# Packed attention and a low-rank mixer on one core: three moves at the change from attention to the products

## The chip, the cores and the metric

The kernel runs on one core of one Trainium2 chip. The core has five engines that work side by side and meet through semaphores: TensorE (PE in the profile; PEld is its loading of weights), VectorE (DVE), ScalarE (ACT), GpSimd (POOL) and SyncE (SP), which here only issues the loads and stores; 16 DMA engines carry these out. The metric is the device time of one execution in microseconds (us).

## The reference

```
p_packed = softmax(p k^T / 8) v             # 8 batches, 8 heads: 32 packed tokens from 576
x        = softmax(q p_packed^T / 8) p_packed   # 576 tokens again, heads side by side: 576 x 512
u        = x + (mix of the tokens of x by U V)  # U 576 x 32, V 32 x 576
out      = u + relu(u w1) w2                # w1 512 x 2048, w2 2048 x 512
```

q, k and v are 8 x 8 x 576 x 64 in float32. U, V, w1 and w2 come as float64; the kernel makes float32 of them on the chip, from the two halves of their bits (`float32_of`, L71 to L82): an absolute value on ScalarE (L77) and four integer operations on VectorE (L78 to L81) for each piece.

## The kernel before

**Products.** Every large product runs as three matmuls on a high and a low part (`mm3`, L84 to L88): high by high, high by low, low by high. So each operand is split: ScalarE writes the high part, VectorE or GpSimd the difference.

**First stage.** The first attention (packed tokens from k and v) runs over 16 units, a unit being one batch and four of its heads (loop at L521). The loop writes for unit i: the turn of the exponentials of unit i-1 and the scores of unit i on TensorE, the loads of `vt` for i+1 and `kx` for i+2, the maximum and exponential, conversions of w1, the product with v for unit i-2 (`a_pack`) and the turn of its result (`a_heads`, unit i-3). Beside it, from unit 4 on, three steps a unit of the second attention of batch 0 (`attention`, L255, a list of 24 steps from `load` to the last `mix2`). U and V are loaded (`load_uv`) and prepared (`prepare_uv`) at units given by two conditions, L544 and L546. At unit 13 stands the first fold of w1 with the packed tokens (`fold`: 16 matmuls, casts L378, differences L379), at unit 14 the loads of w2's first pieces, the `q` loads of batch 1, and the conversion of w2's piece 0. What is written here is put in order by a scheduler that simulates the engines; each engine then works through its own list in that order.

**Second stage.** From L567 on the order is as written. For each batch and each of 16 columns kt: a first product `gemm1` (L86 to L88 into `h_ps`, then ReLU on ScalarE, L619, and the difference `hl` on VectorE, L622), one step of the next batch's attention, the second product `gemm2` of column kt-1 with something in between its halves, every fourth column a fold, and another step. In batch 0 the four remaining pieces of the first attention (`rest`) go in between the halves of columns 1 to 4, and w2 is converted piece by piece while it is used: `split_w2` (cast L160, difference L161), the load of a later piece, `convert_w2`.

What sets the places of batch 1's steps is a list into which empty steps are put:

```
w2x = convert_w2(1)
for n in (20, 19, 18, 15, 15, 14, 13, 12, 12, 11, 5, 0, 0, 0, 0):
    steps.insert(n, lambda: None)
```

**Buffers.** `bank()` hands out two PSUM banks in turn (named `t_ps`), shared by the turns, the scores of the second attention, the folds and `mix1`/`mix2`. `x_tile` has two buffers, used by U and V, by the `q` loads and by the tokens that `mix1` reads; `bits` has two, `vt` three. A new user of a buffer waits until the last reader of the old one is done.

Of the kernel before, what the change touches and what calls it, by code (L numbers as in the profile page):

```python
# [19 lines left out]
def packed_attention_mixer_kernel(  # L20
# [50 lines left out]
    def float32_of(x, t, raw, out=None, tested=False):  # L71


        low, high = raw[:, :, 0], raw[:, :, 1]
        out = x if out is None else out.bitcast(I32)
        if not tested:
            nc.scalar.activation(t, high.bitcast(F32), AF.Abs)  # L77
        nc.vector.tensor_single_scalar(t, t, LEAST, op=ALU.max)  # L78
        nc.vector.tensor_scalar(x, t.bitcast(I32), 3, 0x3FFFFFF8, op0=ALU.logical_shift_left, op1=ALU.bitwise_and)
        nc.vector.scalar_tensor_tensor(x, high, -0x40000000, x, op0=ALU.bitwise_and, op1=ALU.bitwise_or)  # L80
        nc.vector.scalar_tensor_tensor(out, low, 29, x, op0=ALU.logical_shift_right, op1=ALU.bitwise_or)  # L81
        return out.bitcast(F32)  # L82
# [44 lines left out]
    def conv_tile(dtype):  # L127
        return pipe.tile([P, DM], dtype, name="os", bufs=4)
# [7 lines left out]
    def load_w1(n):  # L136
        x, c = chunks[n]
        b = bits["w1", n] = bits_tile() if n % 2 else sA.tile([P, 512, 2], I32, name="bits2")
        nc.sync.dma_start(out=b.rearrange("p x t -> p (x t)"), in_=w1[P * x:P * x + P, 2 * QW * c:2 * QW * c + 2 * QW])
# [15 lines left out]
    def convert_w2(kt):  # L155
        return kt, float32_of(conv_tile(I32), conv_tile(F32), bits.pop(("w2", kt)))
# [238 lines left out]
    def bank_a(tag):  # L395
        return lambda: psA.tile([P, 512], F32, name=f"{tag}_ps", tag=tag)

    def a_load(u):
        b, g = UN[u]
        ua[u] = {}  # L400
        if g == 0:
            pn[b] = sA.tile([P, 2, D], F32, name="pn", bufs=1)
            nc.sync.dma_start(out=pn[b], in_=p[b].rearrange("(g h) n d -> (h n) g d", g=2))
        ua[u]["x"] = sA.tile([P, 2 * S], F32, name="kx", bufs=3)
        load_nat(ua[u]["x"], k, b, g)

    def a_load_v(u):
        b, g = UN[u]
        vt = ua[u]["v"] = sT.tile([P, 5, 4 * D], F32, name="vt", bufs=3)
        rows = v[b, 4 * g:4 * g + 4].rearrange("h (i c) d -> i c h d", c=NT)  # L410
        main = v[b, 4 * g:4 * g + 4].rearrange("h (i c) d -> i h (c d)", c=NT)
        for a in range(2):
            nc.sync.dma_start(out=vt[:, :4].rearrange("(i a) h x -> a i h x", a=2)[a],
                              in_=main[:, :, 4 * D * a:4 * D * a + 4 * D])
        nc.sync.dma_start(out=vt[:64, 4].rearrange("p (h d) -> p h d", h=4), in_=rows[:, 8])
# [13 lines left out]
    def a_turn(u):  # L429
        b, g = UN[u]  # L430
        if g == 0:
            a_p(b)
        ua[u]["t"] = sA.tile([P, 4, 5 * I], F32, name="kT")
        for h in range(3):
            turn(ua[u]["t"], ua[u]["x"], h, bank_a("k"), split=h == 1)

    def a_scores(u):
        b, g = UN[u]
        s_ps = psA.tile([P, 1024], F32, name="s_ps", tag="s", bufs=1)
        scores(pT[b], ua[u]["t"], g, (s_ps[:, 512 - 5 * I:512], s_ps[:, 512:512 + 4 * I]))  # L440
        ua[u]["s"] = s_ps[:, 512 - 5 * I:512 + 4 * I]

    def a_softmax(u):
        b, g = UN[u]
        if g == 0:
            sums[b] = sT.tile([P, 4], F32, name="sm", bufs=3)
        mx = sums[b][:, 2 + g:3 + g]
        nc.vector.tensor_reduce(mx, ua[u]["s"], axis=AX.X, op=ALU.max, negate=True)
        e1 = ua[u]["e"] = sT.tile([P, S], F32, name="e1")
        nc.scalar.activation(e1, ua[u]["s"], AF.Exp, bias=mx, accum_out=sums[b][:, g:g + 1])  # L450

    def a_turn_back(u, bank):
        b, g = UN[u]
        e1 = ua[u]["e"]
        eT = ua[u]["eT"] = sT.tile([P, 5, P], F32, name="eT")
        t_ps = bank()
        for kk in range(4):
            turn_back(t_ps, e1, kk, P * kk)
        nc.scalar.copy(eT[:, :4].rearrange("p k x -> p (k x)"), t_ps)
        t_ps = bank()  # L460
        turn_back(t_ps, e1, 4, 0)
        nc.scalar.copy(eT[:64, 4], t_ps[:64, :P])
        if g == 1 or b == B - 1:
            s = sums[b][:, :2] if b < B - 1 else sums[b][:, g:g + 1]
            nc.scalar.activation(s, s, AF.Identity, bias=eps)
            nc.vector.reciprocal(s, s)
# [16 lines left out]
    def a_heads(u):  # L483
        b, g = UN[u]
        if g == 0:
            pps[b] = ppT_tile() if b == 0 else sT.tile([P, 2, P], F32, name="ppTa")
        z_ps = bank()
        nc.tensor.transpose(z_ps[:, :P], ua[u]["two"].rearrange("p z d -> p (z d)"), ident)
        nc.scalar.copy(pps[b][:, g], z_ps[:, :P])
        if g == 1:  # L490
            if b == 0:
                ppT[0] = pps[0]
            else:
                nc.sync.dma_start(out=ppTd[b], in_=pps[b].rearrange("p g n -> p (g n)"))
# [16 lines left out]
    def some_w1(n):  # L511
        convert_w1(n)
        if n + 1 < 16:
            test_w1(n + 1)
        if n + 4 < 16:
            load_w1(n + 4)
# [4 lines left out]
    for i in range(NU):  # L521
        if i > 0:
            a_turn_back(i - 1, bank_a("m"))
        a_scores(i)
        if i + 1 < NU:
            a_load_v(i + 1)
            a_turn(i + 1)
        if i + 2 < NU:
            a_load(i + 2)
        a_softmax(i)  # L530
        if i < 2:
            load_w1(2 + i)
        for _ in range(turns[i]):
            some_w1(n_w1)
            n_w1 += 1
        if i > 1:
            a_pack(i - 2, bank_a("m"))
        if i > 2:
            a_heads(i - 3)
        if i >= 4:  # L540
            for _ in range(3):
                if first:
                    first.pop(0)()
        if i == 2:  # L544
            uv = load_uv()
        if i == 3:  # L546
            prepare_uv(*uv)
        if i == 13:
            fold(0, 0)
        if i == 14:  # L550
            load_w2(0)
            load_w2(1)
            steps = attention(1, res)
            steps.pop(0)()
            split_w2(*convert_w2(0))
            load_w2(2)
# [130 lines left out]
        for i, queue in enumerate((nc.sync, nc.scalar)):  # L687
            queue.dma_start(out=out[b - 1 + i].rearrange("(i c) m -> c i m", c=NT)[8], in_=os_[I * i:I * i + I])

    w2x = convert_w2(1)  # L690

    for n in (20, 19, 18, 15, 15, 14, 13, 12, 12, 11, 5, 0, 0, 0, 0):
        steps.insert(n, lambda: None)
    last, parts = None, []
    for b in range(B):
        cur = Batch(b)
        oj = None
        ahead = attention(b + 2, res) if b + 2 < B else []
        for kt in range(NK):
            cur.gemm1(kt)  # L700
            if oj and kt == 1:
                store_joint(b - 1, oj)
            if steps and (b < 2 or kt % 4 != 2) and (b, kt) != (1, 0):
                steps.pop(0)()
            if (b, kt) == (0, 5):
                w2_tiles(ctx.enter_context(tc.tile_pool(name="sC", bufs=1, side="right", reuse_waits="tile")), 2)
            if kt > 0:
                cur.gemm2(kt - 1, (rest or steps).pop(0) if b == 0 and (rest or steps) else None)
            elif last:
                last.gemm2(NK - 1)  # L710
                last.store()
                if last.b % 2 == 1:
                    oj = joint(last.b, parts)
            if kt % 4 == 2 and (b, kt) != (B - 1, NK - 2):
                n = b * NPC + kt // 4 + 1
                fold(n // NPC, n % NPC)
            if w2x and kt != 8:
                n = kt + 2 - (kt > 8)
                split_w2(*w2x)
                w2x = None  # L720
                if n + 1 < NK:
                    load_w2(n + 1)
                if n < NK:
                    w2x = convert_w2(n)
            if steps and kt % 4 != 2 and (b, kt) != (1, 0):
                steps.pop(0)()
            if kt == 1:
                cur.blocks()
            if kt == 3:
                cur.add_u()  # L730
            if ahead and kt == (13 if b else NK - 1):
                ahead.pop(0)()
            if kt == NK - 1 and b % 2 == 1:
                parts = [joint_parts(b, 0), joint_parts(b, 1)]
        assert not steps
        steps = ahead
        last = cur
# [35 lines left out]
```

## Time and profile before

| what | value |
|---|---|
| time, median of 3 runs | 840.88 us (840.63 to 841.08) |
| the profiled execution | 841.66 us |
| its span in the profile | 839.4 us |
| TensorE busy | 810.5 us (97%) |
| VectorE, ScalarE, GpSimd busy | 375.8, 332.3, 83.8 us |
| moved by DMA | 58.13 MB, 46.83 of it read from HBM |

The span goes from the first to the last instruction; the profiled execution's own time is 2.26 us longer. PEclk in the rows is the TensorE clock that was granted, as a share of 2.4 GHz; 0.50 is 1.2 GHz. In a row of a timeline the two numbers are start and duration, and what stands in brackets is how long the engine was idle before and who released it. L numbers are lines of the kernel above.

### The profile page before, as it was taken

What the parts mean: (1) busy time and instruction counts of PE and PEld (TensorE: products, weight loads), DVE (VectorE), ACT (ScalarE), POOL (GpSimd) and SP (SyncE); (2) the same over time, 40 slices, a digit from 0 to 9 for tenths busy, and PEclk for the clock granted to TensorE, in tenths of its full rate; (3) what the DMA queues carried; (4) which work ended last, traced back from release to release, by engine and by line L of the source; (5) the groups of instructions that cost most, each with busy time, mean ns of one, the idle gap of its engine ahead of it and who ended that gap; (6) DMA issues with size and microseconds to landing.
All of it is one profiled execution on the core that took longest, in us unless ns stands there. A gap on an engine that the chain in (4) does not pass through costs nothing.

```text
span 839.4 us, 14644 instructions
## 1 busy us (share of the span) xinstructions
PE 810.5 (97%) x5824; PEld 656.3 (78%) x5824; DVE 375.8 (45%) x887; ACT 332.3 (40%) x1046; POOL 83.8 (10%) x123
## 2 busy tenths in 40 slices
PE   8788899999999999999999999999999999999997
PEld 6455587787878887888788887888788887888786
DVE  3888767885243334433344234333434234342222
ACT  5787755444233333333233332343234232332231
POOL 0222401100111001010101001010101011100000
PEclk8999999999999999999999999999999999999999
DMA  9999722231001100011001100110001100010001
GB/s 308 355 356 350 230 82 83 77 136 52 1 1 64 50 14 1 1 64 51 1 1 63 54 11 1 59 55 1 2 25 59 43 1 2 1 51 1 1 1 64
DMA packets 36244, 58.13 MB, mean 69 GB/s; under 512 B 9040, under 2 KB 19280, under 8 KB 36176
## 3 DMA queue, kind: packets, MB, share of 16 engines
q1 hardware_dynamic: 35856, 56.67, 20.1%
q8 instruction: 46, 0.75, 0.4%
q10 hardware_dynamic: 320, 0.52, 0.2%
q14 instruction: 22, 0.18, 0.1%
HBM read 46.83 MB, written 10.35 MB: 68 GB/s over the span
## 4 chain that ended last, share of the span: by engine, by line
PE 87%; DVE 4%; ACT 3%; DMA 2%; issue 1%; POOL 0%; DVEq 0%; SPq 0%
PE o L86 17%; PE o L88 17%; PE o L87 17%; PE h_ps L86 9%; PE h_ps L87 8%; PE h_ps L88 8%; PE t_ps L372 4%; PE t_ps L224 2%; PE t_ps L244 2%; PE t_ps L320 1%; DVE os L80 1%; PE t_ps L250 1%; DMA bits<-in_moe_w_ch_dram 1%; PE t_ps L332 1%; DMA kx<-in_k_dram 1%
## 5 line engine op out<-in xcount | busy, mean ns | idle before, releaser
L86 PE MATMUL o<-w2h,hh 128*128 128x512 f32 x512 | 207.2, 405 | 0.4 <-ACT w2h L160 0.4
L87 PE MATMUL o<-w2l,hh 128*128 128x512 f32 x512 | 202.6, 396 | 0.5 <-DVE w2l L161 0.5
L88 PE MATMUL o<-w2h,hl 128*128 128x512 f32 x512 | 202.7, 396 | 0.0
L622 DVE SCALAR_TENSOR_TENSOR hl<-h_ps,hh 128x256 fp32r<-128x256 f32 x256 | 104.0, 422 | 198.0 <-ACT hj L621 186.0
L619 ACT ACTIVATE hh<-h_ps 128x256 fp32r<-128x256 f32 x256 | 98.7, 387 | 184.5 <-PE h_ps L88 183.9
L86 PE MATMUL h_ps<-ah,wth 128*128 128x320 f32 (+1 forms) x512 | 157.7, 308 | 2.6 <-DVE hl L622 2.6
L87 PE MATMUL h_ps<-al,wth 128*128 128x320 f32 (+1 forms) x512 | 152.1, 297 | 0.5 <-POOL al L335 0.4
L88 PE MATMUL h_ps<-ah,wtl 128*128 128x320 f32 (+1 forms) x512 | 151.7, 296 | 0.0
L86 PEld LDWEIGHTS h_ps<-ah,wth 128*128 128x128 f32 x512 | 96.8, 189 | 34.8 <-issue 27.7
L86 PEld LDWEIGHTS o<-w2h,hh 128*128 128x128 f32 x512 | 97.2, 190 | 21.9 <-issue 4.6
L88 PEld LDWEIGHTS o<-w2h,hl 128*128 128x128 f32 x512 | 96.7, 189 | 22.5
L87 PEld LDWEIGHTS o<-w2l,hh 128*128 128x128 f32 x512 | 97.2, 190 | 18.0 <-DVE w2l L161 1.1
L87 PEld LDWEIGHTS h_ps<-al,wth 128*128 128x128 f32 x512 | 97.1, 190 | 2.6 <-POOL al L335 0.9
L88 PEld LDWEIGHTS h_ps<-ah,wtl 128*128 128x128 f32 x512 | 97.3, 190 | 0.0
L379 DVE TENSOR_TENSOR wtl<-t_ps,wth 128x256 fp32r<-128x256 f32 x128 | 48.5, 420 | 97.4 <-ACT wth L378 94.0
L378 ACT CAST wth<-t_ps 128x256 fp32r<-128x256 f32 x128 | 43.3, 374 | 107.8 <-PE t_ps L372 101.1
L335 POOL TENSOR_TENSOR al<-aT,ah 128x320 fp32r<-128x320 f32 (+1 forms) x32 | 25.7, 805 | 213.0 <-ACT ah L334 213.0
L283 POOL TENSOR_TENSOR e<-e,m 128x576 f32<-128x576 f32 x16 | 18.6, 1163 | 252.0 <-DVE m L282 252.0
L231 ACT COPY xT<-t_ps 128x256 f32<-128x256 f32 x64 | 21.3, 394 | 39.5 <-PE t_ps L224 38.8
L372 PE MATMUL t_ps<-w1t,ppT 64*32 64x512 f32 x512 | 34.9, 601 | 0.0
L334 ACT CAST ah<-aT 128x320 fp32r<-128x320 f32 (+1 forms) x32 | 13.7, 434 | 45.4 <-DVE aT L333 45.4
L294 POOL TENSOR_TENSOR e<-e,s 128x576 f32<-128x576 f32 x16 | 18.6, 1163 | 107.7 <-DVE s L293 107.7
(138 smaller groups left out, 954.6 us busy)
## 6 DMA issues: line engine op xcount, KB each, us to landing
bits<-in_moe_w_ch_dram SPq DMA_DIRECT2D x32, 512.0 KB, 5.7
kx<-in_k_dram SPq DMA_DIRECT2D x16, 576.0 KB, 6.9
x<-in_q_dram SPq DMA_DIRECT2D x16, 576.0 KB, 4.9
vt<-in_v_dram SPq DMA_DIRECT2D x32, 256.0 KB, 7.0
out_dram<-bits SPq DMA_DIRECT2D x32, 256.0 KB, 2.4
vt<-in_v_dram SPq DMA_DIRECT2D x16, 64.0 KB, 6.6
ppTd<-ppTa SPq DMA_DIRECT2D x7, 128.0 KB, 3.8
ppT<-ppTd SPq DMA_DIRECT2D x7, 128.0 KB, 4.7
```

The lines of the kernel that those rows point to most:

```text
L86: nc.tensor.matmul(ps, lhsT=lh, rhs=rh, start=start, stop=False)
L87: nc.tensor.matmul(ps, lhsT=lh, rhs=rl, start=False, stop=False)
L88: nc.tensor.matmul(ps, lhsT=ll, rhs=rh, start=False, stop=stop)
L231: nc.scalar.copy(dst, src[:, a])
L283: nc.gpsimd.tensor_tensor(e, e, m.unsqueeze(2).to_broadcast([P, S // 32, 32]), op=ALU.subtract)
L294: nc.gpsimd.tensor_tensor(e, e, s.unsqueeze(2).to_broadcast([P, S // 32, 32]), op=ALU.mult)
L335: nc.gpsimd.tensor_tensor(al[:, g, ns], aT[:, ns], ah[:, g, ns].bitcast(F32), op=ALU.subtract)
L372: nc.tensor.matmul(f_ps[g][xs], lhsT=ppT[b][zs, g, xs], rhs=w1t[h // 2][zs, QW * c:QW * c + QW], start=True, stop=True)
L378: nc.scalar.copy(hi[:, g], f_ps[g][:, cs])
L379: nc.vector.tensor_tensor(lo[:, g], f_ps[g][:, cs], hi[:, g].bitcast(F32), op=ALU.subtract)
L619: nc.scalar.activation(hh[:, ms], src, AF.Relu)
L622: nc.vector.scalar_tensor_tensor(hl[:, ms], src, 0.0, hh[:, ms].bitcast(F32), op0=ALU.max, op1=ALU.subtract)
```

## The change

U and V are loaded at unit 0 and prepared at unit 1, rather than 2 and 3. The conversion of w2's piece 1 is written behind the first `gemm1` rather than ahead of the loop. Three of the four empty steps at the head of the list go.

```
-        if i == 2:
+        if i == 0:
             uv = load_uv()
-        if i == 3:
+        if i == 1:
             prepare_uv(*uv)
...
-    w2x = convert_w2(1)
-
-    for n in (20, 19, 18, 15, 15, 14, 13, 12, 12, 11, 5, 0, 0, 0, 0):
+    w2x = None
+
+    for n in (20, 19, 18, 15, 15, 14, 13, 12, 12, 11, 5, 0):
         steps.insert(n, lambda: None)
...
             cur.gemm1(kt)
+            if (b, kt) == (0, 0):
+                w2x = convert_w2(1)
```

Batch 0 has 39 places for a step. Before, 38 steps and empty steps fill them; now 35, and the last `mix2` moves from between the halves of column 15 to the first place of column 14.

SP's list near the end of the first stage, before; `bits_1660` is piece 0 of w2, `x_1664` and `x_1666` are the `q` loads of batch 1, `kx`, `vt` and `pn` those of k, v and p:

```order
L213 DMA kx_1508<-in_k_dram 128x2x576
L153 DMA bits_1660<-in_moe_w_ch2_dram 128x1024
L494 DMA ppTd3_77<-ppTa_1112 128x256
L413 DMA vt_1270<-in_v_dram 64x4x256 x2
L415 DMA vt_1270<-in_v_dram 64x4x64
L213 DMA x_1664<-in_q_dram 128x2x576
L213 DMA x_1666<-in_q_dram 128x2x576
L413 DMA vt_1380<-in_v_dram 64x4x256 x2
L415 DMA vt_1380<-in_v_dram 64x4x64
L494 DMA ppTd4_78<-ppTa_1340 128x256
```

And now:

```order
L494 DMA ppTd3_77<-ppTa_1112 128x256
L139 DMA bits_1427<-in_moe_w_ch1_dram 128x1024
L213 DMA kx_1508<-in_k_dram 128x2x576
L213 DMA x_1664<-in_q_dram 128x2x576
L413 DMA vt_1270<-in_v_dram 64x4x256 x2
L415 DMA vt_1270<-in_v_dram 64x4x64
L403 DMA pn_1403<-in_p_dram 128x2x64
L413 DMA vt_1380<-in_v_dram 64x4x256 x2
L415 DMA vt_1380<-in_v_dram 64x4x64
L213 DMA x_1666<-in_q_dram 128x2x576
L153 DMA bits_1660<-in_moe_w_ch2_dram 128x1024
```

The load of w2's piece 0 stood right behind the last `kx`; now both `q` loads and the `vt` of two units stand ahead of it, and a piece of w1 (`bits_1427`) ahead of the `kx`.

VectorE's list at the first product, before; `os` is the piece of w2 in conversion (`bits_1662` is piece 1), `hl` the difference of the first product's ReLU:

```order
L448 TENSOR_REDUCE sm_1614<-s_ps_1693 128x1
L78 TENSOR_SCALAR os_1769<-os_1769 128x512
L79 TENSOR_SCALAR os_1768<-os_1769 128x512
L80 SCALAR_TENSOR_TENSOR os_1768<-bits_1662,os_1768 128x512
L81 SCALAR_TENSOR_TENSOR os_1768<-bits_1662,os_1768 128x512
L622 SCALAR_TENSOR_TENSOR hl_1776<-h_ps0_1777,hh_1775 128x256
L622 SCALAR_TENSOR_TENSOR hl_1776<-h_ps1_1787,hh_1775 128x256
L161 TENSOR_TENSOR w2l0_87<-os_1768,w2h0_86 128x512
L78 TENSOR_SCALAR os_1801<-os_1801 128x512
```

And now:

```order
L448 TENSOR_REDUCE sm_1614<-s_ps_1693 128x1
L622 SCALAR_TENSOR_TENSOR hl_1769<-h_ps0_1770,hh_1768 128x256
L622 SCALAR_TENSOR_TENSOR hl_1769<-h_ps1_1780,hh_1768 128x256
L78 TENSOR_SCALAR os_1790<-os_1790 128x512
L79 TENSOR_SCALAR os_1789<-os_1790 128x512
L80 SCALAR_TENSOR_TENSOR os_1789<-bits_1662,os_1789 128x512
L81 SCALAR_TENSOR_TENSOR os_1789<-bits_1662,os_1789 128x512
L161 TENSOR_TENSOR w2l0_87<-os_1789,w2h0_86 128x512
L78 TENSOR_SCALAR os_1801<-os_1801 128x512
```

The four operations on piece 1 have gone behind the two `hl`.

VectorE's list at column 2, before; `rdl` and `ajl` belong to the batch's own blocks, `sm` is the sum of the last unit of the first attention, `wtl` the second fold:

```order
L601 TENSOR_TENSOR rdl0_1754<-ppall_73,rdh0_1752 32x64 x8
L604 CAST ajl0_1758<-al_1245 128x2x64
L622 SCALAR_TENSOR_TENSOR hl_1902<-h_ps0_1903,hh_1901 128x256
L622 SCALAR_TENSOR_TENSOR hl_1902<-h_ps1_1913,hh_1901 128x256
L466 RECIPROCAL sm_1614<-sm_1614 128x1
L379 TENSOR_TENSOR wtl_1965<-t_ps_1954,wth_1964 128x256
```

And now:

```order
L601 TENSOR_TENSOR rdl0_1754<-ppall_73,rdh0_1752 32x64 x8
L604 CAST ajl0_1758<-al_1245 128x2x64
L622 SCALAR_TENSOR_TENSOR hl_1921<-h_ps0_1922,hh_1920 128x256
L622 SCALAR_TENSOR_TENSOR hl_1921<-h_ps1_1932,hh_1920 128x256
L276 STREAM_TRANSPOSE e_1941<-t_ps_1942 128x320
L277 STREAM_TRANSPOSE e_1941<-t_ps_1943 128x256
L466 RECIPROCAL sm_1614<-sm_1614 128x1
L379 TENSOR_TENSOR wtl_1989<-t_ps_1978,wth_1988 128x256
```

The two that take the scores of batch 1 out of PSUM (L276, L277) have come in ahead of the reciprocal, which belongs to `a_turn_back` of the last unit.

## Rows read from the trace of the kernel before

**Rows 1.** Busy time by stretches: from, to; length; PE, PEld, DVE, ACT, POOL; PEclk; DMA share; GB/s
```profile
0.00:80.00 80.00, 63.54 (x915) 45.03 (x915) 59.33 (x126) 59.14 (x184) 15.76 (x33) 0.96 1.03 340
...
300.00:400.00 100.00, 99.73 (x649) 82.28 (x648) 38.39 (x101) 33.38 (x109) 9.59 (x11) 1.00 0.07 24
```

**Rows 2.** TensorE's waits, 100 to 320 us: us in total, times, longest
```profile
PE h_ps L86 <- DVE hl L622: 2.6, 2, 2.1
PE o L87 <- DVE w2l L161: 0.5, 2, 0.2
PE h_ps L87 <- POOL al L335: 0.4, 1, 0.4
PE o L86 <- ACT w2h L160: 0.4, 1, 0.4
```

**Rows 3.** Timeline around the longest of these waits
```profile
98.58 0.39 ACT L619 ACTIVATE hh<-h_ps 128x256 fp32r<-128x256 f32 x1
...
98.63 0.43 DVE L78 TENSOR_SCALAR os<-os 128x512 f32<-128x512 f32 x1 [1.70 <-ACT os L77]
...
100.28 0.69 DVE L81 SCALAR_TENSOR_TENSOR os<-bits,os 128x512 int32<-128x512 int32 x1
100.89 0.75 DVE L622 SCALAR_TENSOR_TENSOR hl<-h_ps,hh 128x256 fp32r<-128x256 f32 x2
...
101.36 0.41 PE L86 MATMUL h_ps<-ah,wth 128*128 128x320 f32 x1 [2.10 <-DVE hl L622]
```

**Rows 4.** Busy time by stretches, behind that wait
```profile
102.00:106.00 4.00, 4.00 (x16) 3.30 (x14) 3.17 (x7) 1.09 (x4) 0.00 (x0) 0.57 0.34 133
106.00:107.00 1.00, 1.00 (x42) 0.73 (x42) 0.00 (x0) 0.00 (x0) 0.00 (x0) 1.00 0.00 0
```

**Rows 5.** Busy time by stretches, at the end of the full stretch
```profile
80.00:88.00 8.00, 7.12 (x102) 4.30 (x101) 4.48 (x12) 6.43 (x23) 2.63 (x5) 1.00 1.06 368
88.00:92.00 4.00, 4.00 (x87) 2.54 (x85) 3.73 (x8) 3.93 (x15) 1.24 (x3) 1.00 0.52 142
```

**Rows 6.** Timeline of SP, its last load of that stretch
```profile
84.08 1.24 SPq L415 DMA_DIRECT2D vt<-in_v_dram  x1
```

**Rows 7.** DMA issues at 84 to 86 and 92 to 94: KB each, us to landing
```profile
vt<-in_v_dram SPq DMA_DIRECT2D x1, 64.0 KB, 6.7
...
bits<-in_moe_w_ch_dram SPq DMA_DIRECT2D x2, 512.0 KB, 4.8
```

**Rows 8.** Timeline of the conversion of w2's first piece and the last maximum
```profile
87.97 0.70 ACT L77 ACTIVATE os<-bits 128x512 f32<-128x512 f32 x1
...
88.70 0.59 DVE L78 TENSOR_SCALAR os<-os 128x512 f32<-128x512 f32 x1 [0.23 <-ACT os L77]
...
92.21 0.67 DVE L81 SCALAR_TENSOR_TENSOR w1t<-bits,os 128x512 int32<-128x512 int32 x1
...
96.18 0.75 DVE L448 TENSOR_REDUCE sm<-s_ps 128x1 f32<-128x576 f32 x1
```

**Rows 9.** Costliest groups: operation xcount; busy, mean ns of one; idle before, releaser
```profile
L379 DVE TENSOR_TENSOR wtl<-t_ps,wth 128x256 fp32r<-128x256 f32 x128 | 48.5, 420 | 97.4 <-ACT wth L378 94.0
```

**Rows 10.** The loads into `bits`, 84 to 112 us
```profile
DMA to landing us min/median/max: 3.4/3.7/5.2
```

**Rows 11.** SP's waits over the span: us in total, times, longest
```profile
SPq L213 <- PE t_ps L320: 10.8, 5, 3.1
```

**Rows 12.** Busy time by stretches, in the first stage
```profile
68.00:72.00 4.00, 3.09 (x67) 2.15 (x69) 3.97 (x9) 3.82 (x11) 2.28 (x3) 1.00 1.04 338
```

**Rows 13.** Timeline of columns 2 to 4
```profile
111.05 1.50 DVE L601 TENSOR_TENSOR rdl<-ppall,rdh 32x64 fp32r<-32x64 f32 x8
...
113.92 1.09 PE L372 MATMUL t_ps<-w1t,ppT 64*32 64x512 f32 x16
...
124.30 0.31 PE L86 MATMUL h_ps<-ah,wth 128*128 128x320 f32 x1
...
126.86 0.51 DVE L276 STREAM_TRANSPOSE e<-t_ps 128x320 f32<-128x320 f32 x1
```

## The prediction

> **What bounds the kernel now.** I read four views in this order. First the busy time by stretches [rows 1]: from 0 to 80 us the DMA engines are full (share 1.03) at 340 GB/s, so the attention stage goes at the pace of its loads; from 300 to 400 us TensorE is busy 99.73 of 100 us, so in the product stage the time is TensorE's work plus its waits. Second, who made TensorE wait from 100 to 320 us [rows 2]: four lines, 3.9 us together, and 2.1 us of that is one wait for `hl`. Third, the instructions around that wait [rows 3]: ScalarE starts the first product's ReLU at 98.58, but VectorE, which works in program order, first turns the second piece of w2 into float32 (98.63 to 100.97) and takes `hl` from PSUM only at 100.89; TensorE's next product starts at 101.36. Behind that wait the granted clock fell: its mean from 102 to 106 us is 0.57, that is nearly all of it at 1.2 GHz, and from 106 on it is 1.00, 2.4 GHz [rows 4]. At 0.57 the 4 us hold the work of 2.3, so 1.7 us are lost. Fourth, SP's queue and the DMA engines around the change of stage [rows 5, 6]: 368 GB/s from 80 to 88 us and 142 from 88 to 92, so the full stretch ends near 89.5 us, and the first ReLU follows some 9 us later. What is loaded last there, and what must be done with it, counts.
>
> The profiled execution took 841.66 us (span 839.4 and 2.26 around it), 0.78 above the median of the runs, 840.88. The sum is made against 841.66 and then lowered by 0.78.
>
> **Part 1, U and V two units sooner.** No instruction is added or removed. ScalarE's, VectorE's and TensorE's work for them moves ahead by two units, on engines that are busy 74, 74 and 79% of the first 80 us. The loads set the pace there, so I count nothing for it directly: the cover is the full DMA queue of [rows 1]; without that cover it would still come out at nothing, since what is late two units sooner is early two units later. The scheduler, though, writes the whole attention stage in a new order, and one consequence has a price. SP's rows in the section on the change show the load of w2's first piece (`bits_1660`) moved from behind the last `kx` to behind both `q` loads of the second batch and two `vt` sets. One copy of 128 KB and four times 576 KB, 2.49 MB, stand ahead of it that stood behind; at 368 GB/s [rows 5] that is 6.8 us later. It is now the last load of the full stretch (the `vt` sets behind it wait for their buffers). Today the last one is the 64 KB of `vt` issued at 84.08, which took 6.7 us, so to 90.8 [rows 6, 7]. I take 90.3 for `bits_1660`, between the end of the full stretch and that landing.
>
> Who waits for it: ScalarE's absolute value (L77), and queued behind that, in order, the exponential of unit 14, the casts of the first fold and the last exponential; on VectorE its conversion stands ahead of the four differences `wtl` and of the last maximum. From arrival on: L77 0.7; two conversions written into each other, which took from 88.70 to 92.88 with a foreign copy of 0.4 in between, so 3.8; four L379 at 0.42, 1.7; about 0.4 until the fourth cast has been done; and from the last maximum to the first ReLU 2.4 (96.18 to 98.58), less the 0.7 of L77 on the second piece, which goes, plus 0.3 for a small copy (`ppTa`) that now stands behind the exponential. That is 8.6 us [rows 3, 8, 9]. So the first ReLU can start at 98.9, against 98.58 now: +0.3 us, and an arrival of 90.0 would be even. Today this L77 ran at 87.97 on data that had been asked for before both `q` loads, so today the engines and not the load set the chain. Bounds: arriving by 88.7, and with nothing else in the way, the chain allows 97.3, -1.3 us. If SP stands still ahead of it, because its first `q` load waits for the first batch's `mix1` before two `vt` sets are issued, the longest wait of that kind, 3.1 us [rows 11], would come on top: +3.4.
>
> The next two pieces of w2 are late too. They reuse the two buffers that these conversions read, as they do now, so with two of the four `wtl` written into the conversions they are asked for 0.7 + 3.8 + 0.8 = 5.3 us behind 90.3, at 95.6. A piece took 4.8 us to land when asked for among other loads, 3.7 in the median from 84 to 112 us [rows 7, 10]; with 4.2 the second one lands at 99.8, and ScalarE wants it behind the first product's ReLUs, 0.7 behind 98.9, at 99.6: 0.2 us late (bounds 0 and 0.8).
>
> By the Trainium skill ("DMA: Bandwidth & Descriptors", Specifications) a core's share of HBM is about 358 GB/s; by it the 30.1 MB that are in by 88 us could be in after 84, the piece would not be late, and the sum would be 0.3 us lower. The trace decides otherwise: 340 GB/s over 80 us and then 368 give 27.2 and 2.9 MB, and the second figure is above the page's [rows 1, 5].
>
> **Part 2, the second piece of w2 behind the first product.** One absolute value on ScalarE and four conversion instructions on VectorE move behind the two `hl` evictions. VectorE then takes `hl` right behind the ReLU, and the wait of 2.1 us goes. On SP the load that reuses these bits stands behind the conversion in either order. What is late next is VectorE itself, since the same conversions now run later against TensorE, and part 3 decides where that shows.
>
> **Part 3, three empty places less.** The second attention's `turn_q` go to columns 0 and 1 and its first `scores_q` to column 2. That is TensorE work moved, none added. But `scores_q` takes both shared PSUM banks just ahead of `a_turn_back`, and VectorE has to empty them (L276, L277, in the third order fence), behind the conversion of another piece of w2, eight small `rdl` instructions and `hl`. Counted from the start of the first ReLU on, each from the same instructions before: the ReLU, both evictions and L77 1.4; conversion 2.3 (98.63 to 100.97); cast and hand-over 0.7; difference 0.6; conversion 2.3; two `hl` 0.7; difference 0.6; conversion 2.3; `rdl` and `ajl` 1.6; two `hl` 0.75; L276 0.5: 13.8 us [rows 3, 13]. TensorE comes to `a_turn_back` at about 12.4: its work up to there, and an estimated 1.7 us of waits before it for banks that ScalarE empties behind the cast of w2's second piece (two, 1.3 and 0.4 us). There it waits some 1.4 us. From that point to the first product of column 4 it is as long as now, 11.5 us: 10.4 from the fold (113.92 to 124.30), less a `turn_q` of 0.75 that has gone ahead, plus 1.9 for the turn and half a product before the fold [rows 13]. The first product of column 4 then starts 13.8 + 11.5 = 25.3 us behind the first ReLU. Now it is 124.30 - 98.58 = 25.7 [rows 3, 13], with `scores_q`, 0.7 us of TensorE, still to come. Gain 0.4 + 0.7 = 1.1 us.
>
> The second piece's 0.2 us goes into this chain: 0.9 is left. So of the 2.1 us of waiting and the 1.7 at half clock I let 0.9 through; the rest goes into new waits for PSUM banks. Upper bound 3.8 (VectorE is never late), lower bound -0.6 (all of it comes back, the clock falls again, and only `scores_q` is hidden). I take 0.9 since it is counted from rows. On the clock the row shows one wait of 2.1 us with a fall behind it; the new waits are shorter each, and a fall between the first two of them and `a_turn_back` would be paid out of the 1.4 us that TensorE waits there anyway.
>
> At the end of the first batch `mix2` comes in column 14 rather than between the halves of column 15, so that `al` is there when the second batch starts: the wait of 0.4 us for it [rows 2] goes. Bounds 0 and 0.7.
>
> **Sum.** +0.3 - 0.9 - 0.4 = -1.0: 840.66 for an execution like the profiled one, **839.9 us** against the median. The other waits, 0.9 us for w2's parts and 0.5 for `hl` [rows 2], can move either way.
>
> **Rivals.**
> - *Attention ends sooner.* For: U and V are out of the way of VectorE two units earlier, and it is full later, 3.97 of 4 us from 68 to 72 [rows 12]. Against: the DMA engines are full there too (1.04), and w2's first piece stands at the end of their work. If the piece comes by 88.7, the first ReLU is 1.3 us sooner and the rest as above: -1.3 - 1.3 = -2.6, 838.3 us.
> - *Slower: w2's first piece comes late.* Place: SP's queue at the first `q` load, which waits for `mix1`; each microsecond of arrival beyond 90.0 is one of first ReLU. It eats the 1.3 us gained from an arrival of 91.3 on, and from 93.0 on the loss can be told. With the 3.1 us of [rows 11] on 90.3 the arrival is 93.4 and the sum -1.3 + 3.4 = +2.1: 843.0 us. Against: the loads issued before it take some 6.7 us to land, which hides a short stop of SP.
> - *The change doesn't do what it says:* the wait goes whole from `hl` to the PSUM banks, and only the delays of the loads are left: +0.3 + 0.2 = +0.5, 841.4 us.
>
> **How the numbers follow.** Forecast 0.45, sooner attention 0.26, late piece 0.18, wait only moved 0.11. A measurement of this kernel can tell about 0.2% (1.7 us) from no change. Faster by more than that: 0.22 of the second case and 0.11 of the first, 0.33. Slower by more: 0.13 of the third, 0.05 of the others, 0.18. Within: 0.49. The range for 8 in 10 reaches from below the sooner case (837.8) to short of the late one's middle (842.8); the forecast's own range is 838.8 to 841.5.
>
> **What would show it.** Right: no wait of TensorE for `hl` between the first and the second product; TensorE waiting 1 to 2 us at the `a_turn_back` of column 2 for L276; L77 on `bits_1660` starting as that lands, near 90; the first ReLU at 98.5 to 99.5; no wait for `al` at the second batch. Wrong: a first ReLU before 98 or after 101, a wait in columns 1 to 3 above 2 us with a granted clock of 0.50 behind it for longer than now, or waits that appear only after column 4.

## The result, and the profile after

The changed kernel is slower: 845.14 us in the median (843.49 to 847.25, 9 runs) against 841.08 for the kernel before, timed beside it (840.30 to 843.32, 9 runs). The ratio is 1.0040, its 95% interval 1.0027 to 1.0053: 3.4 us lost by the ratio, 4.1 between the medians, where 1 us of gain was forecast, and outside the range given. The profiled execution took 846.17 us, span 844.1.

TensorE's waits after, from 100 to 320 us, answer to [rows 2] (columns as there):

```profile
PE h_ps L86 <- DVE hl L622: 1.4, 2, 0.9
PE t_ps L250 <- DVE e L276: 1.3, 1, 1.3
PE t_ps L478 <- ACT xT L231: 0.9, 1, 0.9
PE t_ps L372 <- DVE aT L333: 0.7, 1, 0.7
PE o L87 <- DVE w2l L161: 0.4, 2, 0.2
PE t_ps L488 <- ACT xT L231: 0.3, 1, 0.3
```

The wait of 2.1 us for `hl` between the first and the second product is gone (two others remain, 1.4 us together), and the waits for PSUM banks are there with nearly the sizes that the prediction gave: 1.3 us for L276 (1.4 was said), 0.9 and 0.3 for banks that ScalarE empties (1.3 and 0.4). A wait of 0.7 us at a fold (L372) was not foreseen. Together they are 5.0 us, against 3.9 before.

The larger part of the loss comes ahead of that. SP's issue of w2's first piece after, its landing, and ScalarE and VectorE from there to the first ReLU (answering to [rows 3] and [rows 6 to 8]):

```profile
86.41 0.35 SPq L153 DMA_DIRECT2D bits<-in_moe_w_ch_dram  x1
```
```profile
bits<-in_moe_w_ch_dram SPq DMA_DIRECT2D x1, 512.0 KB, 5.6
```
```profile
93.75 0.73 ACT L77 ACTIVATE os<-bits 128x512 f32<-128x512 f32 x1
94.17 0.76 DVE L448 TENSOR_REDUCE sm<-s_ps 128x1 f32<-128x576 f32 x1 [2.58 <-PE s_ps L244]
...
100.51 0.75 DVE L448 TENSOR_REDUCE sm<-s_ps 128x1 f32<-128x576 f32 x1
...
102.49 0.38 ACT L619 ACTIVATE hh<-h_ps 128x256 fp32r<-128x256 f32 x1
```

The first ReLU starts at 102.49, 3.9 us later than before. From 80 to 88 us the DMA engines, as full as before, moved 321 GB/s and not 368 (after, answering to [rows 5]):

```profile
80.00:88.00 8.00, 7.06 (x106) 4.08 (x107) 7.39 (x16) 7.01 (x25) 2.86 (x4) 1.00 1.05 321
```

The piece landed at 92.0, 1.7 us later than assumed; SP had also stood still from 84.41 to 85.69, ahead of the second `q` load and so of the piece behind it. But L77 has no wait in front of it: ScalarE came to it only at 93.75, out of its own list. The busy time between the maxima of the last four units shows where the time lies. After (maximum of unit 12 to 13, 13 to 14, 14 to 15, and on to the first ReLU; columns as in [rows 1]):

```profile
84.29:88.50 4.21, 3.42 (x65) 1.99 (x63) 4.21 (x11) 3.96 (x12) 1.80 (x3) 1.00 1.04 277
88.50:94.17 5.67, 4.74 (x95) 3.25 (x98) 2.23 (x5) 4.59 (x18) 2.28 (x5) 1.00 0.77 262
94.17:100.51 6.34, 3.37 (x78) 1.47 (x62) 5.77 (x13) 4.15 (x12) 1.34 (x3) 1.00 0.47 116
100.51:102.49 1.98, 1.89 (x13) 1.85 (x10) 0.75 (x2) 1.20 (x5) 1.98 (x6) 0.62 1.01 383
```

The same four stretches of the kernel before:

```profile
84.43:87.71 3.28, 2.83 (x29) 1.44 (x29) 2.15 (x6) 3.28 (x11) 1.81 (x5) 1.00 1.05 361
87.71:92.80 5.09, 5.09 (x122) 3.38 (x121) 4.82 (x11) 4.76 (x18) 1.53 (x3) 1.00 0.64 190
92.80:96.18 3.38, 2.04 (x46) 1.00 (x34) 2.25 (x8) 2.88 (x11) 1.83 (x3) 1.00 0.89 268
96.18:98.58 2.40, 2.26 (x49) 1.96 (x50) 0.75 (x2) 2.39 (x8) 2.40 (x8) 1.00 1.04 369
```

Unit 12's maximum comes at the same time in these two executions (84.29 and 84.43). From there to the first ReLU it is 18.20 us now and was 14.15, and the largest piece is the stretch between the last two maxima: 6.34 against 3.38 us, with VectorE busy 5.77 against 2.25, since both last conversions (w2's first piece, w1's last) now stand there with the fold's four differences. Unit 15's scores were done by then, and VectorE came to their maximum late: 3.2 us after their end, against 0.9 before. After, then before:

```profile
96.55 0.76 PE L244 MATMUL s_ps<-kT,pT 64*32 64x320 f32 x16
```
```profile
94.47 0.77 PE L244 MATMUL s_ps<-kT,pT 64*32 64x320 f32 x16 [1.21 <-ACT e L450]
```

TensorE is idle for nearly half of the stretch, and behind that its clock falls (after):

```profile
96.00:100.00 4.00, 1.96 (x46) 1.02 (x49) 3.63 (x9) 2.53 (x8) 0.81 (x1) 1.00 0.35 79
100.00:104.00 4.00, 3.91 (x48) 3.66 (x37) 1.51 (x3) 2.23 (x9) 3.59 (x10) 0.62 0.78 288
```

So the half clock that the prediction let go with the `hl` wait [rows 4] is back: TensorE stood still ahead of the first product instead of behind it, and 0.62 granted over 4 us (mostly 1.2 GHz) is 1.5 us lost, nearly the 1.7 of before. From the first to the last L621 (one a column, 128 of them) the second stage took 718.49 us (102.77 to 821.26), 0.79 more than before.

### The profile page after: what moved, and what is told of

Same layout as the page of the kernel before. It is cut to its first block, busy times and chain, and to the rows that moved or that the text cites. A ratio compares the mean times of both kernels' runs of the same rounds, so it can differ in the third digit from the quotient of the medians.

```text
span 844.1 us, 14631 instructions
## 1 busy us (share of the span) xinstructions
PE 815.8 (97%) x5824; PEld 658.4 (78%) x5824; DVE 378.3 (45%) x887; ACT 332.2 (39%) x1046; POOL 85.5 (10%) x123
## 4 chain that ended last, share of the span: by engine, by line
PE 85%; DVE 7%; ACT 3%; DMA 2%; issue 2%; SPq 0%; POOL 0%; DVEq 0%; ACTq 0%
PE o L86 16%; PE o L88 16%; PE o L87 16%; PE h_ps L86 8%; PE h_ps L88 8%; PE h_ps L87 8%; PE t_ps L372 4%; DMA bits<-in_moe_w_ch_dram 2%; PE t_ps L224 1%; PE t_ps L244 1%; DVE os L80 1%; PE t_ps L320 1%; PE t_ps L250 1%; DVE os L78 1%; DMA kx<-in_k_dram 1%
## 5 line engine op out<-in xcount | busy, mean ns | idle before, releaser
L335 POOL TENSOR_TENSOR al<-aT,ah 128x320 fp32r<-128x320 f32 (+1 forms) x32 | 26.9, 843 | 213.3 <-ACT ah L334 213.3
L372 PE MATMUL t_ps<-w1t,ppT 64*32 64x512 f32 x512 | 36.0, 601 | 0.7 <-DVE aT L333 0.7
```

Source lines behind the costliest of these rows:

```text
L335: nc.gpsimd.tensor_tensor(al[:, g, ns], aT[:, ns], ah[:, g, ns].bitcast(F32), op=ALU.subtract)
L372: nc.tensor.matmul(f_ps[g][xs], lhsT=ppT[b][zs, g, xs], rhs=w1t[h // 2][zs, QW * c:QW * c + QW], start=True, stop=True)
```

## The experiments

Ratios are to the kernel before, timed beside each, with their 95% intervals. "Second stage" is the time from the first to the last L621 in the profiled execution, against that of before. "Tail" is unit 12's maximum to the first ReLU. "Places" are the empty places at the list's head.

**The change taken apart.** First part 1 alone:

```
-        if i == 2:
+        if i == 0:
...
-        if i == 3:
+        if i == 1:
```


> Only U and V two units sooner; the second stage is written as before. Theory A, the loss was made in the attention stage, whose order the scheduler wrote anew: the first ReLU starts near 102.5 us as in the changed kernel (98.6 before) and the time is 3 to 4.5 us above before, about 844.9. Rival B, the loss comes from the new order meeting the two edits at the second stage: the first ReLU still late but most of it absorbed by the old waits, time within 1.5 us of before.

844.03 us, ratio 1.0026 (1.0013 to 1.0040). First ReLU at 100.97, tail 19.56 us, its stretches 4.21, 5.67, 6.34 and 3.34. By the ratio that is 2.2 us above before, between the 3 to 4.5 of theory A and the 1.5 of rival B: more than half of the loss is made in the attention stage, as theory A has it, and not all of it. In this profile L77 did wait for the load:

```profile
91.27 0.69 ACT L77 ACTIVATE os<-bits 128x512 f32<-128x512 f32 x1 [0.26 <-DMA bits<-in_moe_w_ch_dram]
```

It was 0.26 us, and the stretches around it are as long as in the changed kernel, where it did not wait.

Parts 2 and 3 alone (the attention stage is then, list by list, that of before):

```
-    w2x = convert_w2(1)
+    w2x = None
...
-    for n in (20, 19, 18, 15, 15, 14, 13, 12, 12, 11, 5, 0, 0, 0, 0):
+    for n in (20, 19, 18, 15, 15, 14, 13, 12, 12, 11, 5, 0):
...
+            if (b, kt) == (0, 0):
+                w2x = convert_w2(1)
```


> Only the second piece of w2 behind the first product and three empty places less; the attention stage is in the order of before. By the working of the prediction (wait of 2.1 us and half clock partly kept as waits for PSUM banks): 1.3 us faster than before, about 839.8. Rival: what the changed kernel's trace shows from the first ReLU on, 0.8 us slower, is made by these two edits alone: about 841.9. If the 0.8 came from TensorE's idle time ahead of the first product, this kernel is at or below before.

843.25 us, 1.0013 (1.0003 to 1.0024). Second stage 0.20 us longer. At column 6, where the first scores are done in both, it was 0.87 us ahead, as the working had it (0.9); from there to the second batch it lost 1.07. Its clock stays at 1.00 from 96 to 108 us. By the ratio the two edits cost 1.1 us, and the profile shows only 0.2 of it (its tail is that of before, 14.17 us); where the rest lies is not shown.

Part 2 alone, and part 3 alone (each the lines above that belong to it):

> Only the second piece of w2 behind the first product; the empty places as before. If the wait of 2.1 us for hl was worth something alone: 1 to 3 us faster, 838 to 840. If VectorE is then late for the next product instead: within 0.5 us of before.

> Only three empty places less; w2's second piece ahead of the first product as before. If the wait of a_turn_back for the scores' way out of PSUM (L276) costs time: 0.5 to 1.5 us slower, about 842. If it lies in the shadow of what VectorE owes anyway: within 0.5 us of before, with the wait for al at the second batch gone, 840.7 to 841.3.

The piece alone: 841.15 us, 0.9992 (0.9980 to 1.0004), second stage 1.65 us shorter, its clock 1.00 from 100 to 104 us. The places alone: 843.10 us, 1.0016 (1.0003 to 1.0029), second stage 0.25 longer. So of the two edits one helps in the trace (too little to be told in the time) and the other costs, more in the time (1.3 us by the ratio) than in the trace.

**What in part 3 costs.** All three have the piece's move. Only the turns sooner; turns and first scores sooner; everything sooner but the last `mix2`:

```
+    for n in (20, 19, 18, 15, 15, 14, 13, 12, 12, 11, 5, 3, 3, 3, 0):
```


> U and V as before, w2's second piece behind the first product; the three empty places are taken from ahead of the second attention's turns and put behind them, ahead of its first scores: turn_q in columns 0 and 1, everything from scores_q on as before. The two edits at the second stage cost 1.9 us against the piece's move alone. If the waits for banks that ScalarE empties (1.1 and 0.3 us, L231) are the turns' own: about 1.2 us above the piece's move alone, 0.3 above before. If they come only with the scores in column 2: as the piece's move alone, 0.9 below before.


```
+    for n in (20, 19, 18, 15, 15, 14, 13, 12, 12, 11, 5, 5, 5, 5, 0):
```


> U and V as before, w2's second piece behind the first product; turns and scores of the second attention three places sooner, everything behind the first softmax1 as before. If the scores in column 2 are what costs (wait for L276, 1.3 us, behind the conversion of piece 3): about 1.3 us above the kernel with only the turns sooner (which was 0.8 below the piece's move alone), so 0.4 to 0.6 above the piece's move alone. If the cost lies at the end of the batch (the fold's wait of 0.7 us for aT): as with only the turns sooner.


```
+    for n in (22, 22, 22, 20, 19, 18, 15, 15, 14, 13, 12, 12, 11, 5, 0):
```


> U and V as before, w2's second piece behind the first product, all steps three places sooner as in the changed kernel but for the last mix2, which stands where it stood before. If the fold's wait of 0.7 us for aT comes from the last mix2's new place: that wait gone, that for al (0.4) back, time 0.3 us below the two edits of the second stage together. If it comes from the earlier mix2 steps: wait of 0.7 still there and that of 0.4 added.

Turns sooner: 839.95 us, 0.9977 (0.9965 to 0.9989), second stage 2.41 us shorter; better than expected, as the waits for `hl` fell to 0.5 us. With the scores as well: 0.9993 (0.9983 to 1.0003), 0.95 shorter, and the wait that the prediction named is there:

```profile
PE t_ps L250 <- DVE e L276: 1.3, 1, 1.3
PE t_ps L478 <- ACT xT L231: 1.1, 1, 1.1
PE h_ps L86 <- DVE hl L622: 0.5, 1, 0.5
PE o L87 <- DVE w2l L161: 0.5, 2, 0.2
PE h_ps L87 <- POOL al L335: 0.4, 1, 0.4
...
```

With `mix2` in its old place: 1.0005 (0.9993 to 1.0016), 0.60 shorter, and no wait at the fold. So the scores in column 2 cost 1.46 us and the last `mix2` ahead of the fold 0.80 (against 0.20 longer for the two edits whole).

**U and V at other units,** with the piece's move and the places as before: units 0 and 1, units 0 and 0, units 0 and 3.

```
+        if i == 0:          # prepare_uv at i == 1, 0 or 3
             uv = load_uv()
```


> The changed kernel with its three empty places put back: U and V at units 0 and 1, w2's second piece behind the first product. Theory, the tail: the new order is about 2.5 us sooner than before up to the maximum of unit 12, but holds both last conversions (w2's first piece and w1's last) between the maxima of units 14 and 15, 6.3 us apart rather than 3.4; first ReLU 101 to 102.5, time 2 us above the kernel with the piece's move alone (0.9 below before), so 1 to 1.5 us above before. Rival: the loss of the changed kernel came from the empty places, then at or below before.

> U and V loaded and prepared both at unit 0, w2's second piece behind the first product, empty places as before. Here the scheduler puts both last conversions ahead of the maximum of unit 14, nearly as in the kernel before. Theory, the tail: the maxima of units 14 and 15 are 3.4 to 4 us apart again, first ReLU 2 to 4 us sooner than with units 0 and 1, time 1 to 3 us below before, 839 to 841. Rival, the load of U and V ahead of the first units costs the stream of loads: unit 12's maximum no sooner than before and the time as with units 0 and 1 or worse, 843 or more.

> U and V loaded at unit 0 and prepared at unit 3, w2's second piece behind the first product, empty places as before. Both last conversions stand ahead of the maximum of unit 13 or beside it, only the four differences stand between the last two maxima. Theory, the tail: the last two maxima are at most 3.4 us apart and the first ReLU comes 2 to 4 us sooner than with units 0 and 1; time 1 to 3 us below before. Rival, what counts is when U and V are prepared: then no sooner than before at unit 12, and the time that of the piece's move alone, 0.9 below before.

843.35 us (1.0011, 1.0000 to 1.0021), 840.62 (0.9976, 0.9966 to 0.9985) and 846.47 (1.0050, 1.0033 to 1.0066). The same instructions, three orders, 5.8 us apart. The second's time and first ReLU came as expected. The first was nearly as slow as expected, but its first ReLU came at 103.38, later than the 101 to 102.5 given. The third did not come as expected: its last stretch is short (3.76 us), but unit 12's maximum comes only at 89.23.

**What holds the tail** with units 0 and 1. w1's last conversion one unit sooner (with it the last but two); three of four operations left out on w2's first piece, then also on w1's last; the fold a unit sooner, then that with both shortened:

```
-    turns = [0, 0] + [1] * 10 + [2, 1, 2, 1]
+    turns = [0, 0] + [1] * 10 + [2, 2, 2, 0]
```


> U and V at units 0 and 1, w2's second piece behind the first product, empty places as before, and w1's last piece written one unit sooner. The lists are those of units 0 and 1 but for one thing: that conversion stands ahead of unit 14's maximum, so only one conversion stays between the last two maxima. Theory, the engines' lists set the tail: the last two maxima come 4.0 to 4.5 us apart rather than 6.34, first ReLU 1.5 to 2.2 us sooner after unit 12's maximum, time 1.5 to 2 us below units 0 and 1 with the piece's move (0.1% above before), so 0.1% below before. Rival, the late load of w2's first piece sets the tail: the interval shrinks by less than 0.5 us and the time stays.


```
+        if short: return ...    # out = (low >> 29) | high, ahead of L78
```


> Leaves out three of VectorE's four operations on w2's first piece (1.55 us), all loads and all else as with U and V at units 0 and 1 and w2's second piece behind the first product. Theory, VectorE's work between the last two maxima sets the tail: these come 4.6 to 5.0 us apart rather than 6.34, first ReLU 1.3 to 1.7 us sooner after unit 12's maximum. Rival, the late load sets it: the load is where it was, so the first ReLU stays within 0.4 us at 18.2 to 19.6 us behind unit 12's maximum.

> Leaves out three of VectorE's four operations on w2's first piece and three of the four on w1's last (3.1 us together); one operation of each is left, that of w1 ahead of unit 14's maximum. The loads, TensorE's list and nearly all of ScalarE's stay. Theory, VectorE's work between the last two maxima: these come 3.2 to 3.8 us apart, as before (3.38), first ReLU 2.5 to 3.1 us sooner after unit 12's maximum than with the whole conversions (18.2 to 19.6), time 2 to 3 us lower, 0.1 to 0.25% below before. Rival, the late load: interval and time as with the whole conversions, 0.1% above before.


```
-        if i == 13:
+        if i == 12:
             fold(0, 0)
```


> U and V at units 0 and 1, w2's second piece behind the first product, empty places as before, and the first fold written one unit sooner, at unit 12: its four differences then stand ahead of unit 14's maximum, the two whole conversions stay between the last two maxima. Theory, two chains lie in that interval, the conversions (4.0 us of VectorE) and the fold's casts and differences in turn (3 us): with one out, 14 to 15 takes 4.8 to 5.2 us rather than 6.34, unit 12's maximum to first ReLU 17 to 18.2. Rival, the load of w2's first piece: 6 us or more still.

> The same, and it leaves out three of VectorE's four operations on w2's first piece and on w1's last (the load of w2's first piece stays where it is, late). Theory, both chains out of the last interval: the last two maxima 3.2 to 3.8 us apart, unit 12's maximum to first ReLU 15 to 16.5 us (18.2 to 19.6 with both in), time 0.15 to 0.35% below units 0 and 1 with the piece, at or below before. Rival, the late load or TensorE's order: 5 us or more for the interval, time as before or above.

| kernel | unit 12's max | to 13 | to 14 | to 15 | to ReLU | tail | ratio (interval) |
|---|---|---|---|---|---|---|---|
| before | 84.43 | 3.28 | 5.09 | 3.38 | 2.40 | 14.15 | |
| six others in its order | 84.30 to 87.25 | 3.3 | 5.1 | 3.4 | 2.4 | 14.15 to 14.18 | |
| changed | 84.29 | 4.21 | 5.67 | 6.34 | 1.98 | 18.20 | 1.0040 (1.0027 to 1.0053) |
| part 1 alone | 81.41 | 4.21 | 5.67 | 6.34 | 3.34 | 19.56 | 1.0026 (1.0013 to 1.0040) |
| units 0, 1 and the piece | 84.54 | 4.21 | 5.66 | 6.34 | 2.63 | 18.84 | 1.0011 (1.0000 to 1.0021) |
| w1's last sooner | 84.87 | 4.21 | 5.68 | 5.13 | 3.07 | 18.09 | 1.0014 (1.0002 to 1.0026) |
| w2's first shortened | 84.94 | 4.21 | 5.67 | 6.41 | 2.42 | 18.71 | 1.0015 (1.0004 to 1.0026) |
| both shortened | 82.31 | 5.36 | 5.66 | 5.02 | 2.77 | 18.81 | 1.0014 (1.0004 to 1.0025) |
| fold sooner | 83.35 | 4.21 | 7.26 | 6.29 | 1.77 | 19.53 | 1.0012 (1.0001 to 1.0023) |
| fold sooner, both shortened | 82.29 | 5.35 | 6.74 | 4.06 | 2.46 | 18.61 | 1.0006 (0.9993 to 1.0018) |
| units 0, 0 and the piece | 85.14 | 4.63 | 4.51 | 3.12 | 2.18 | 14.44 | 0.9976 (0.9966 to 0.9985) |

None of the five shortened the tail as its theory had it. (The fold sooner has the 6 us or more that its rival gave for the last stretch, but its L77 came at 96.68 and waited for no load.) That VectorE's work alone sets the tail falls. With 3.1 us of it left out the last stretch shrinks to 5.02 and with the fold away to 4.06, but the others grow, and the tail stays between 18.1 and 19.6 us in all eight kernels with U and V at units 0 and 1 and p of the last batch where it was. VectorE's list does hold the last maximum: in seven of the eight, unit 15's scores are done 1.9 to 3.3 us before VectorE takes their maximum. The edits are not pure, since the scheduler writes the lists anew for each: with w2's first piece shortened, its cast (L160) comes ahead of the fold's casts on ScalarE, and one L81 takes 1.65 us beside GpSimd where it has 0.68 in the changed kernel:

```profile
97.03 1.34 POOL L161 TENSOR_TENSOR w2l<-os,w2h 128x512 fp32r<-128x512 f32 x1 [2.19 <-ACT w2h L160]
97.28 1.65 DVE L81 SCALAR_TENSOR_TENSOR w1t<-bits,os 128x512 int32<-128x512 int32 x1
```

The wait for the late load falls too as the one cause: in seven of the eight, ScalarE's absolute value on w2's first piece (L77, L76 where operations are left out) did not wait for it. In the last row of units 0 and 1, fold sooner and both shortened, VectorE is idle ahead of both maxima and waits for TensorE's scores:

```profile
94.38 0.76 DVE L448 TENSOR_REDUCE sm<-s_ps 128x1 f32<-128x576 f32 x1 [2.54 <-PE s_ps L244]
...
98.44 0.76 DVE L448 TENSOR_REDUCE sm<-s_ps 128x1 f32<-128x576 f32 x1 [1.91 <-PE s_ps L244]
```

**The lists of TensorE and ScalarE.** In the order of units 0 and 1 the turn of the last batch's p (L423), which unit 14's scores need, stands behind the product with v (L478), and that behind unit 13's exponential. From the changed kernel, ScalarE and TensorE between the maxima of units 13 and 14:

```profile
89.28 0.74 ACT L450 ACTIVATE e<-s_ps,sm 128x576 f32<-128x576 f32 x1
```
```profile
90.16 0.66 PE L250 MATMUL m_ps<-ident,e 128*128 128x128 f32 x4 [0.33 <-ACT e L450]
...
91.66 0.90 PE L478 MATMUL m_ps<-vt,eT 128*32 128x64 f32 x40 [0.34 <-ACT eT L459]
92.49 0.44 PE L423 MATMUL t_ps<-ident,pd 128*128 128x128 f32 x2
...
93.30 0.77 PE L244 MATMUL s_ps<-kT,pT 64*32 64x320 f32 x16 [0.26 <-ACT pT L424]
```

Exponential, turn, copy, product, turn of p, copy, scores, maximum: one behind the other, most of them handed from one engine to another. In the kernel before, L423 runs at 88.45, ahead of the product, and unit 14's scores at 90.58. The same split runs through all traces: from unit 13's maximum to unit 14's it is 4.2 to 5.1 us in the eleven where the turn of p stands ahead of the products, 5.7 to 7.3 in the nine where it stands behind them. That holds for this stretch and not for the last one. To bring that order back I loaded the last batch's p earlier; the second kernel has the turns of part 3 too:

```
+        if i == 8: nc.sync.dma_start(out=ppall[:, B - 1], in_=p[B - 1]...)
```


> U and V at units 0 and 1, w2's second piece behind the first product, empty places as before, and one load of 64 KB moved: p of the last batch is loaded at unit 8 into the place that its packed tokens use later, rather than behind a q load and a set of vt. With that the scheduler writes the turn of p (L423 in the others) ahead of the product with v and the first fold's casts around unit 14's exponential, as in the kernel before; w2's first piece is loaded sooner too. Theory, the serial order at the end of the attention stage costs the time: unit 12's maximum to first ReLU 14.0 to 14.8 us rather than 18.2 to 19.6, time 2 to 3 us below units 0 and 1 with the piece (0.1% above before), 0.15 to 0.3% below before. Rival, U and V at units 0 and 1 themselves cost it, by their loads and work ahead: time within 1 us of units 0 and 1 with the piece.

> The same with the second attention's turns in columns 0 and 1 and its scores where they were before. The second stage 0.75 us shorter than without; 0.25 to 0.35% below before.

843.54 us, 1.0016 (1.0003 to 1.0030), and 843.44, 1.0014 (0.9998 to 1.0031). The tail did shrink, to 16.18 and 16.17 us (14.0 to 14.8 expected), but unit 12's maximum came at 89.78 and 88.08, so nothing was won. SP's queue shows one delay: the last `kx` waits behind the copy of packed tokens (L495 in this kernel), which stood still for 4.4 us.

```profile
75.89 0.34 SPq L139 DMA_DIRECT2D bits<-in_moe_w_ch_dram  x1
80.69 0.34 SPq L495 DMA_DIRECT2D ppTd<-ppTa  x1
81.73 0.38 SPq L213 DMA_DIRECT2D kx<-in_k_dram  x1
```

But that `kx` is unit 15's. Unit 12's scores (88.39) stand behind the turn of their own p (87.20), and GpSimd's copy for it (L422 here) stood behind another one that waited 10.7 us for ScalarE:

```profile
83.95 0.24 POOL L482 COPY ppall<-two 128x64 f32<-128x64 f32 x1 [10.72 <-ACT two L481]
84.12 0.40 POOL L422 COPY pd<-pn 128x256 f32<-128x256 f32 x1
```

Which of the two made unit 12 late was not tried.

**The two gains together,** units 0 and 0 and the turns sooner:

> The two that gained put together: U and V both at unit 0, w2's second piece behind the first product, turns of the second attention in columns 0 and 1 with its scores where they were. If the gains add: the second stage 0.75 us shorter than with U and V at unit 0 and the piece alone, 839.9, 0.3% below before. If the turns' two waits for banks (1.1 and 0.3 us) meet other work: no better than 840.6.

840.27 us, 0.9974 (0.9965 to 0.9983); second stage 2.45 us shorter, tail 14.42. It beats both kernels, but the 0.8 us that the turns win in the trace are not told apart in the time from each gain alone (units 0 and 0: 0.9976; turns: 0.9977).

## Why the prediction was wrong

- *What bounds the kernel.* Right for the second stage; the reading of the first (its loads set the pace, VectorE's and TensorE's order costs nothing) did not hold: with the same loads in another order, unit 12's maximum came anywhere from 81.41 to 89.78 us (one execution each), and behind it the order of the engines' lists cost 4 us and more.
- *Part 1, the step that failed:* the new order of the attention stage was priced at nothing ("so I count nothing for it directly") but for one late load: "So the first ReLU can start at 98.9, against 98.58 now: +0.3 us". It measured +3.9 in the profile, and part 1 alone cost 2.2 us (1.0026). Two things went wrong in it. The arrival was 92.0 and not 90.3, as the stretch from 80 to 88 us moved 321 GB/s and not 368 and SP stood still for 1.3 us. And the chain was counted from that arrival on, as if all else waited for it, with every other list as before. The chain's length was about right (8.7 us from L77 to ReLU, 8.6 said), but L77 came 1.75 us after the landing, and leaving out most of what the chain counts didn't shorten the tail.
- *What stands in its place:* from unit 12's maximum to the first ReLU the new order is 4.0 to 5.4 us longer (changed kernel, part 1 alone, units 0 and 1 with the piece), and the three stretches between the maxima are alike to 0.01 us in these three. Ahead of it the order gains: unit 12's maximum comes at 83.5 in the mean of the eight kernels in that order and at 85.4 in that of the seven in the order of before, one execution of each: 1.9 us. For part 1 alone that makes 5.4 - 1.9 - 0.9 (its second stage) = 2.6 us by the traces, against 2.2 in the time. Behind unit 12 the traces show two holders, the turn of p behind the products up to unit 14's maximum and VectorE's list up to unit 15's. That either causes the loss was argued from the traces and not shown: the one order that brought p's turn forward moved unit 12.
- The figure of 358 GB/s (the Trainium skill, "DMA: Bandwidth & Descriptors", Specifications) played no part: the stream was below it where it mattered, and the landing did not set the time.
- *The rival "sooner attention"* was there up to unit 12 (1.9 us in the mean, above), and more than that was lost behind it.
- *The rival "late piece"* had the right sign and about half the size (+2.1), by another mechanism: SP did not stand still at the first `q` load, and the landing did not decide.
- *Part 2:* the wait for `hl` went, and alone the edit gave 1.65 us in the trace, about the half clock of [rows 4] that the sum was unsure of. In the changed kernel the half clock came back, behind TensorE's idle time ahead of the first product; parts 2 and 3 alone, behind the attention stage of before, kept 1.00 from 96 to 108 us.
- *Part 3:* up to column 6 the working was right (0.87 us gained, 0.9 said). The term "-0.4" for `al` was wrong: the last `mix2` now stands ahead of a fold that needs the bank which VectorE empties (L333), and 1.07 us were lost there and around it, 0.80 of it with the last `mix2`'s place.
- *Sum:* -1.0 forecast, +3.4 measured by the ratio; part 1 alone +2.2 and parts 2 and 3 alone +1.1, together 3.3.

## What to carry to other kernels

Where a scheduler writes the order, a move of a few instructions early on is a new order everywhere: compare the lists of all engines at the end of the stage, at the places where the engines hand over to each other, and not only the queue in which a difference strikes the eye. A chain counted from one late arrival is a lower bound as long as the other lists are not read. And when a stage ends on a fixed resource (here the loads until about 89 us), work that is done sooner within it can be lost again in the order of its last units: here some 1.9 us won up to unit 12, 4 and more lost behind it.

## What had not been expected

The tail is rigid: seven profiled executions in the order of before have 14.15 to 14.18 us from unit 12's maximum to the first ReLU, while that maximum itself lies between 84.30 and 87.25 us. So the scatter of these kernels (840.2 to 844.3 us for the kernel before) has at least one source in the part bound by loads; what makes it there was not tried. An order can be without it: with U and V both at unit 0 twelve executions lie between 840.13 and 841.22 us, and the kernel before, timed beside them, between 840.45 and 844.30. The fastest are 0.3 us apart, so most of that order's gain is that the late executions are missing.

VectorE's short operations grow beside GpSimd. In the changed kernel:

```profile
89.17 0.97 DVE L78 TENSOR_SCALAR os<-os 128x512 f32<-128x512 f32 x1
```
```profile
94.85 0.42 DVE L78 TENSOR_SCALAR os<-os 128x512 f32<-128x512 f32 x1
```
```profile
86.86 2.99 POOL L335 TENSOR_TENSOR al<-aT,ah 128x320 fp32r<-128x320 f32 x3 [2.41 <-ACT ah L334]
```

The first L78 starts while GpSimd's L335 runs (until 89.85) and takes 0.97 us, the second alone 0.42. One more L78 of the changed kernel (83.28, 1.09 us) and one of the kernel before (88.70, 0.59 us) overlap an L335; all three end 0.29 to 0.30 us after GpSimd does, whenever they started. The Trainium skill ("SBUF — State Buffer", SBUF: two separate sides) says that the two share a pair of ports which one instruction holds whole; the rows agree with it: L78's end goes by GpSimd's, which costs 0.55 us here.
